# A retention layer with a gated feed-forward network on one core: fewer, wider column blocks in the middle of the feed-forward loop

## The chip, the core and the metric

The kernel runs on one core of a Trainium2 chip. The core has a matrix engine (TensorE, PE in the profile; its weight loads are PEld), three elementwise engines (VectorE is DVE, ScalarE is ACT, GpSimd is POOL), and a sync engine (SP) whose queue issues nearly all the DMAs. [...] The metric is the device time of one execution in microseconds.

## What is computed

Two layers, one fed into the other. First a retention layer: 8 batches, 8 heads, 576 positions, head size 64. Then a gated feed-forward network on its output, taken as 4608 rows (tokens) of 512 features, with 1536 hidden features.

```python
scores = scale * np.matmul(q, k.transpose(0, 1, 3, 2))
Dmat   = np.where(rel >= 0, gamma[:, None, None] ** rel[None, :, :], 0.0)
attn   = np.matmul(scores * Dmat[None, :, :, :], v)        # no softmax
x      = attn.transpose(0, 2, 1, 3).reshape(B * S, H * D)  # 4608 x 512
gate   = 1.0 / (1.0 + np.exp(-(x @ w_gate)))
out    = (gate * (x @ w_val)) @ w_out                      # 4608 x 512
```

Since there is no softmax, the retention layer is done chunk by chunk with a running state. The work within a chunk is a small masked product, and everything before the chunk enters through the state (the sum of k times v so far).

## The kernel before

**Columns.** The result of the retention layer is kept transposed in `xT`: 4 tiles of 128 features by 4608 columns, one column a token. Everything downstream counts in columns. Columns 0 to 768 are made by a special first part (three "pairs" of chunks). It also runs the feed-forward network on columns 0 to 512. The rest is done by the loop at the end of the kernel (lines 786 to 802), and that loop is what the change touches.

**The retention layer as steps.** The columns from 768 on are made by 34 steps, numbered from 0 (`STEPS`, line 68). A step is one chunk of one batch: 128 columns, or 64 for the last chunk of a batch ("short"; 576 is four chunks of 128 and one of 64). Steps 0 and 1 are full, 2 and 3 short, then each batch has four full ones and a short one. Step 4 begins at column 1152, step 7 at 1536, step 12 at 2112.

Each step has a supply side, which doesn't use TensorE:

- `load` (L105): v, k and q of the chunk come from memory, three DMAs on the SP queue.
- `cast_k` (L252), `cast_q` (L262), `cast_v` (L273), all on POOL: q and k are scaled by the decay tables and cast to bf16 into `qk_nat`, v into `vbd`. There are four of each buffer.
- `cross` (L289): a transposing DMA on the SP queue turns `qk_nat` into `T`, which holds q and k with the head dimension on partitions.

And it has a TensorE side of three or four **phases**: `st0` and `st1` add to the state (L432, not in a short step), `qk` makes the scores from `T` (L399), `pv` makes the output (L418 with the state, L420 within the chunk). DVE masks the scores (L401) and casts the state (L438). ACT casts the result into `xT` (L422) and prepares v (L283).

The order of the SP queue is written out by hand in `casts_to`: for each step x first the loads of step x + 1 (x + 2 from step 12 on), then, after the casts of k and q, the transpose of step x. The queue issues them in just this order.

**The feed-forward network as blocks.** `BLOCKS` (L786) cuts the columns from 512 on into blocks. For a block of n columns, `ffn_units` yields small units of TensorE work. In `h_units`, for each of 12 groups of hidden features there are four matmuls of n columns with the gate weights and four with the value weights (L495). ACT takes the sigmoid and DVE multiplies (L509 and L511 up to 256 columns, where gate and value share one PSUM buffer and are one unit; L519 and L523 above, with a buffer and a unit each). In `op_units`, for each 128 columns, 12 matmuls of 512 columns with the output weights (L561) follow in three units of four. ACT copies the result out (L538), and its store is issued once ten results are waiting. The PSUM ring for all of this has three buffers.

**How the two are interleaved.** While block w is computed, the loop puts in the phases that make the columns of block w + 1, since all of them must be in `xT` before block w + 1 can begin:

```python
end = upto(last_step(nxt[0] + nxt[1])) if nxt else len(order)
todo = end - at
total = 2 * NFC * 4 * n + 12 * 512 * (n // P)
...
    advance(begin + min(todo, -(-todo * gone // (total - 3 * 2048))))
```

`todo` is the number of phases due in this block. After each unit, `gone` of `total` matmul columns have been issued, and phases are let through in proportion, so that the last one comes shortly before the block ends. `order` is the fixed list of phases. It begins st0 0, qk 0, st1 0, pv 0, st0 1, qk 1, st1 1, qk 2, pv 1, qk 3, pv 2, pv 3, st0 4, qk 4 and so on. So the list of blocks sets two things: how many matmuls the hidden layer takes, and how early each phase stands in TensorE's stream. In the kernel before, the first block has the first 9 of these phases in it (up to pv 1), the second the next 11.

Of the kernel before, what the change touches and what calls it, by code (L numbers as in the profile page):

```python
# [16 lines left out]
def kernel(  # L17
# [22 lines left out]
    NT, DM = out.shape  # L40
# [489 lines left out]
    def leave():  # L530
        r, ob = stores.pop(0)
        for p0, r0, w in rows(r, P):
            nc.sync.dma_start(out[r0:r0 + w, :], ob[p0:p0 + w])
# [47 lines left out]
    def upto(s):  # L581

        return order.index(("pv", s)) + 1

    def last_step(t1):
        return max(s for s in range(NS) if at_col[s] < t1)
# [196 lines left out]
        nc.vector.memset(t, 0.0)  # L783
    casts_to(1)

    BLOCKS = [(512, 256), (768, 256)] + [(t, 384) for t in range(1024, 2560, 384)]  # L786
    BLOCKS += [(t, 512) for t in range(2560, NT, 512)]
    pieces = 0
    for w, (t0, n) in enumerate(BLOCKS):
        nxt = BLOCKS[w + 1] if w + 1 < len(BLOCKS) else None  # L790
        end = upto(last_step(nxt[0] + nxt[1])) if nxt else len(order)
# [4 lines left out]
        for cols in ffn_units(t0, n):  # L796
            gone += cols
            pieces += 1
            if stores and (nxt is None or w + 2 == len(BLOCKS) and pieces % 4 == 0):
                leave()  # L800
# [33 lines left out]
```

## Time and profile before

The median of three runs is 337.31 us (337.24 to 337.34). The profiled execution spans 335.4 us.

| engine | busy us | share | what most of it is |
|---|---|---|---|
| PE | 328.0 | 98% | L495 hidden layer, 960 matmuls; L561 output layer, 372 |
| POOL | 185.2 | 55% | L252 73.3 us, L273 47.4, L262 35.4: the casts of the steps |
| ACT | 167.8 | 50% | L519 52.2, L283 41.9 |
| DVE | 164.2 | 49% | L523 59.6, L438 43.7 |

The median of the transposing DMAs takes 4.3 us from issue to landing, that of the loads of k 4.6. Matmuls overlap in the pipeline: a matmul of 384 columns is listed with a mean near 330 ns, though the next one starts about 162 ns later. So the time that a matmul costs is read from the distance between starts, in the timeline, and not from its listed duration; and a PE that is busy 98% of the span isn't thereby known to be free of short waits.

The blocks can be found in the timeline of PE by the size of the L495 matmuls. The block at column 512 starts at 55.75 us, the one at 768 at 73.39, the ones of 384 columns at 91.44, 118.00, 144.5 and 169.7, and the first of 512 columns at 197.58.

### The profile page before, as it was taken

The numbers are of one execution on the slowest core, as the hardware profiler recorded it, in microseconds if no ns is written. First come the engines' busy times: TensorE is split into PE (matmuls) and PEld (weight loads), VectorE is DVE, ScalarE is ACT, GpSimd is POOL, SyncE is SP. The second block draws the span as 40 slices with busy tenths as digits, with TensorE's granted clock in tenths as the row PEclk, the third lists the DMA queues.
The fourth block names the chain that finished last, engine by engine and source line by source line (L and its number), as shares of the span: only waits on it lengthen the run. The fifth ranks groups of instructions, "written<-read, shape, count | busy, mean of one in ns | idle before, by whom it ended". The sixth has DMA issues, their size and how long they took to land.

```text
span 335.4 us, 7396 instructions
## 1 busy us (share of the span) xinstructions
PE 328.0 (98%) x2784; PEld 184.3 (55%) x2784; DVE 164.2 (49%) x328; ACT 167.8 (50%) x345; POOL 185.2 (55%) x327
## 2 busy tenths in 40 slices
PE   7999999999999999999999999999999999999996
PEld 3544445969666566556566555445555455444443
DVE  5744755726376356436346635542574156503320
ACT  6545635637565456355456655445646455233321
POOL 5655679779868798882448966582577500000000
PEclk9999999999999999999999999999999999999999
DMA  7999996799999999999976999499773850020002
GB/s 210 313 372 359 335 255 131 139 225 201 174 214 193 186 205 211 214 247 214 225 132 125 185 240 199 106 232 247 136 135 82 254 203 2 0 95 33 0 31 96
DMA packets 164100, 60.00 MB, mean 179 GB/s; under 512 B 144480, under 2 KB 156000, under 8 KB 164064
## 3 DMA queue, kind: packets, MB, share of 16 engines
q1 hardware_dynamic: 163920, 59.39, 83.2%
q8 instruction: 22, 0.36, 0.5%
q10 hardware_dynamic: 144, 0.13, 0.1%
q14 instruction: 14, 0.11, 0.1%
HBM read 37.75 MB, written 9.44 MB: 141 GB/s over the span
## 4 chain that ended last, share of the span: by engine, by line
PE 94%; DMA 2%; DVE 1%; SPq 1%; issue 1%; ACT 0%; POOL 0%
PE h L495 49%; PE op L561 24%; PE op L745 3%; PE hg L610 3%; PE hv L610 3%; PE pv L420 2%; PE qk L399 2%; PE pv L418 2%; DMA k32p<-in_k_dram 2%; PE st L432 2%; SPq L114 1%; PE op L551 1%; PE pvp L370 1%; PE idle L159 1%; PE st L345 0%
## 5 line engine op out<-in xcount | busy, mean ns | idle before, releaser
L495 PE MATMUL h<-xT,wg_sb 128*128 128x384 bf16 (+2 forms) x480 | 102.8, 337 | 0.2 <-DVE gv L523 0.2
L495 PE MATMUL h<-xT,wv_sb 128*128 128x384 bf16 (+2 forms) x480 | 102.8, 337 | 0.0
L252 POOL TENSOR_TENSOR qk_nat<-k,ktab 64x256 bf16<-64x256 f32 x120 | 73.3, 611 | 42.9 <-PE st L432 27.5
L523 DVE TENSOR_TENSOR gv<-g,h 128x384 bf16<-128x384 bf16 (+1 forms) x96 | 59.6, 621 | 71.8 <-PE h L495 56.4
L561 PE MATMUL op<-wo_sb,gv 128*128 128x512 bf16 x372 | 85.5, 379 | 0.0
L519 ACT ACTIVATE g<-h 128x384 bf16<-128x384 f32 (+1 forms) x96 | 52.2, 544 | 64.9 <-PE h L495 58.3
L438 DVE CAST sbd<-st 64x256 bf16<-64x256 f32 x104 | 43.7, 420 | 45.1 <-PE st L432 42.9
L495 PEld LDWEIGHTS <-wg_sb 128*128 128x128 bf16 x480 | 43.7, 98 | 31.4 <-issue 0.4
L495 PEld LDWEIGHTS <-wv_sb 128*128 128x128 bf16 x480 | 44.1, 98 | 29.0 <-issue 0.4
L273 POOL CAST vbd<-v 64x256 bf16<-64x256 f32 x120 | 47.4, 395 | 15.2 <-PE pv L420 10.6
L561 PEld LDWEIGHTS <-gv 128*128 128x128 bf16 x372 | 34.4, 98 | 36.3
L538 ACT COPY ob<-op 128x512 f32<-128x512 f32 x33 | 19.3, 585 | 47.5 <-PE op L561 42.8
L283 ACT CAST vs<-v 64x256 bf16<-64x256 f32 x104 | 41.9, 403 | 1.6
L262 POOL TENSOR_TENSOR qk_nat<-q,qtab 128x512 bf16<-128x512 f32 (+1 forms) x34 | 35.4, 1041 | 2.6
L422 ACT CAST xT<-pv 128x512 bf16<-128x512 f32 (+1 forms) x34 | 18.1, 534 | 18.1 <-PE pv L420 18.0
L401 DVE TENSOR_TENSOR pt<-qk,tri 128x512 bf16<-128x512 f32 (+1 forms) x34 | 21.2, 625 | 6.1 <-PE qk L399 5.8
L420 PE MATMUL pv<-pt,vbd 128*128 128x64 bf16 x240 | 18.0, 193 | 0.0
L432 PEld LDWEIGHTS <-qk_nat 128*128 128x128 bf16 x208 | 13.2, 98 | 8.8
L420 PEld LDWEIGHTS <-vbd 128*128 128x128 bf16 x240 | 15.2, 98 | 3.5
L418 PE MATMUL pv<-T,sbd 128*128 128x64 bf16 x216 | 17.2, 193 | 0.0
L511 DVE TENSOR_TENSOR gv<-g,h 128x256 bf16<-128x256 bf16 x24 | 10.0, 420 | 13.7 <-ACT g L509 13.3
L418 PEld LDWEIGHTS <-sbd 128*128 128x128 bf16 x216 | 15.1, 98 | 2.5
(76 smaller groups left out, 232.8 us busy)
## 6 DMA issues: line engine op xcount, KB each, us to landing
out_dram<-ob SPq DMA_DIRECT2D x34, 256.0 KB, 2.8
v<-in_v_dram SPq DMA_DIRECT2D x26, 256.0 KB, 4.1
k<-in_k_dram SPq DMA_DIRECT2D x26, 256.0 KB, 4.6
q<-in_q_dram SPq DMA_DIRECT2D x26, 256.0 KB, 5.1
wg<-in_moe_w_gate_dram SPq DMA_DIRECT2D x12, 256.0 KB, 6.0
wv<-in_moe_w_val_dram SPq DMA_DIRECT2D x12, 256.0 KB, 5.8
wo<-in_moe_w_out_dram SPq DMA_DIRECT2D x12, 256.0 KB, 5.4
k32p<-in_k_dram SPq DMA_DIRECT2D x6, 256.0 KB, 5.6
```

The source lines that it names most:

```text
L252: nc.gpsimd.tensor_tensor(out=kn[half(hh), j, :, half(hh)], in0=k32[half(j), hh::2, :], in1=ktab[half(j), c, hh::2].unsqueeze(2).to_broadc ...
L262: nc.gpsimd.tensor_tensor(out=qs[0:n], in0=q32[0:n], in1=qtab[0:n, c, :].unsqueeze(2).to_broadcast([n, H, D]), op=ALU.mult)
L273: nc.gpsimd.tensor_copy(out=vb[half(hh), j, :, half(hh)], in_=v32[half(j), hh::2, :])
L283: nc.scalar.copy(out=natural["vs", s][half(hh), j], in_=loaded[s][0][half(j), hh::2, :])
L401: nc.vector.tensor_tensor(out=pt[:, :, 0:n].rearrange("p m (j t) -> p m j t", t=64), in0=qkp[:, :, 0:n].rearrange("p m (j t) -> p m j t", ...
L418: nc.tensor.matmul(pvp[:, m, half(j)], lhsT=before[:, m, :], rhs=qT[:, m, half(j)], start=True, stop=False)
L420: nc.tensor.matmul(pvp[:, m, half(j)], lhsT=vb[:, j, m, :], rhs=pt[:, m, half(j)], start=before is None, stop=True)
L438: nc.vector.tensor_copy(out=sb[half(hh), :, half(hh)], in_=st_tiles[b][half(hh)])
L495: nc.tensor.matmul(out, lhsT=w_sb[:, kc, fc * P:(fc + 1) * P], rhs=xT[:, kc, t0 + a:t0 + e], start=(kc == 0), stop=(kc == NKC - 1))
L519: nc.scalar.activation(out=g[:, 0:n], in_=h1[:, 0:n], func=AF.Sigmoid)
L523: nc.vector.tensor_tensor(out=gvs[some[0]][:, a:e], in0=g[:, 0:n], in1=h2[:, 0:n], op=ALU.mult)
L561: nc.tensor.matmul(opp, lhsT=gvs[fc][:, nb * P:(nb + 1) * P], rhs=wo_sb[:, fc, :], start=(fc == 0), stop=(fc == NFC - 1))
```

## The change

The list of blocks is cut differently. Columns 768 to 2560 were one block of 256 and four of 384. Now they are two of 384 and two of 512. The block at 512 keeps its 256 columns, and from 2560 on both lists have the same four blocks of 512. The number of blocks falls from ten to nine. Wider blocks mean that each loaded weight tile is used for more columns, so the hidden layer takes fewer matmuls and weight loads, and ACT and DVE fewer instructions for the same columns. No other line is changed, and what is computed stays the same.

```diff
-    BLOCKS = [(512, 256), (768, 256)] + [(t, 384) for t in range(1024, 2560, 384)]
-    BLOCKS += [(t, 512) for t in range(2560, NT, 512)]
+    BLOCKS = [(512, 256), (768, 384), (1152, 384)] + [(t, 512) for t in range(1536, NT, 512)]
```

Since the loop takes the phases of block w + 1 into block w, the change also moves phases: the unchanged first block now has to let through all phases up to column 1152, where it was 1024.

## The prediction

> **What bounds the kernel now.** I read the page's busy times first. They put TensorE at 98% and every other engine near half:
>
> ```profile
> PE 328.0 (98%) x2784; PEld 184.3 (55%) x2784; DVE 164.2 (49%) x328; ACT 167.8 (50%) x345; POOL 185.2 (55%) x327
> ...
> PE   7999999999999999999999999999999999999996
> ```
>
> Next, the waits of PE alone, from 56 us (the first block of the loop) to 332. The answer has a single line:
>
> ```profile
> PE h L495 <- DVE gv L523: 0.2, 1, 0.2
> ```
>
> So in 276 us PE waits visibly once. Going by distances between starts in the PE timeline, small hesitations too short for this list add up to some 0.7 us. From 56 us on the kernel takes as long as PE needs to issue its matmuls; only fewer matmul cycles, or new waits, can move the end.
>
> Then I asked how close the other engines are to making PE wait. A `qk` phase needs its transpose `T`. PE's timeline around steps 1 and 2:
>
> ```profile
> 64.66 0.40 PE L399 MATMUL qk<-T 128*128 128x64 bf16 x8
> ...
> 66.64 0.28 PE L432 MATMUL st<-vs,qk_nat 128*128 128x64 bf16 x4
> ...
> 67.63 0.28 PE L399 MATMUL qk<-T 128*128 128x64 bf16 x4
> 67.75 1.89 PE L561 MATMUL op<-wo_sb,gv 128*128 128x512 bf16 x8
> ```
>
> The SP queue's timeline has the transposes of steps 2 and 3, with the loads between them:
>
> ```profile
> 61.98 1.69 SPq L105 DMA_DIRECT2D q<-in_q_dram  x1
> 63.78 1.28 SPq L289 DMA_TRANSPOSE T<-qk_nat  x1
> 65.11 0.59 SPq L105 DMA_DIRECT2D v<-in_v_dram  x1
> ...
> 67.87 1.73 SPq L289 DMA_TRANSPOSE T<-qk_nat  x1
> ```
>
> The DMA view of a window that holds one of these at a time gives 3.6 us to landing for step 2 and 4.1 for step 3. `T` of step 2 therefore lands at 63.78 + 3.6 = 67.4, and its `qk` starts at 67.63: **0.26 us to spare**, and nothing in the waits shows it. In the same way: steps 0 and 1 land at 57.1 and 62.65 (3.8 us each; used 57.61 and 64.66), step 3 at 71.95 (used 74.27), step 4 at 78.44 (79.38), step 5 at 83.6 (84.57), step 6 at 90.1 (93.50).
>
> Does PE hold this supply back? POOL's timeline says no:
>
> ```profile
> 62.93 0.83 POOL L273 CAST vbd<-v 64x256 bf16<-64x256 f32 x2
> 65.45 1.28 POOL L252 TENSOR_TENSOR qk_nat<-k,ktab 64x256 bf16<-64x256 f32 x2 [1.70 <-DMA k<-in_k_dram]
> ```
>
> From 49.5 to 63.8 us POOL casts without a gap; then it waits for the k of step 3, which was issued behind the transpose of step 1 at 61.34 and took 4.0 us. The next wait, 1.51 us before 70.12, is listed under PE pv L420, but the k load issued at 65.75 lands 4.2 us later, at 69.95, so I read it as the load again. The supply is a loop of SP issue, load, casts, issue, and up to step 12 it runs at its own pace.
>
> **What the Trainium skill says.** "TensorE: Matmul & The Clock Gate", section "Wait — 56ns, not 53.3ns?": a matmul of N columns takes N / 2.4 GHz plus about 2.5 ns, 215.7 ns at 512. The trace agrees: eight of 256 columns take 0.872 us (56.74 to 57.61), 109.0 ns each; four of 384 0.650, 162.5 each; four of 512 0.863, 215.8. Same page, "Step-by-step: what each phase is for": only weight loads are pulled ahead, matmuls "stay in program order". So a `qk` without its `T` stops the hidden-layer matmuls behind it; the trace before has no such stop to check it on. "DMA: Bandwidth & Descriptors", "Anatomy of one DMA — SWDGE (gpsimd) path": semaphore waits are served on the issuing sequencer, before dispatch. The trace agrees for SP: from 57.2 to 58.85 it issues nothing, waiting for POOL's q cast of step 1, though the loads of step 3 stand behind this transpose (issued from 60.35).
>
> **The change, part by part.**
>
> *Fewer matmuls.* Columns 768 to 2560 take 96 hidden-layer matmuls a block: five blocks before, four after. Before: 96 x (109.0 + 4 x 162.5) ns = 72.86 us. After: 96 x (2 x 162.5 + 2 x 215.8) = 72.63. **Gain 0.23 us.** The output layer (14 x 12 matmuls of 512) and the phases are the same ones. Weight loads (98 ns each, beside the matmuls), and the 12 sigmoids and 12 multiplies saved, lie beside PE at half load: nothing.
>
> *Phases earlier in the first block.* It has 18 units of 2048 columns, total 36864, so after unit u ceil(todo x u / 15) phases are through. todo goes from 9 to 12 (up to pv 3). Before, this puts qk 0, 1, 2 behind units 2, 9 and 12, as the timeline shows. After: qk 0, 1, 2, 3 behind units 2, 7, 9 and 12. From the start at 55.75, with 0.872 a unit (0.863 in the output layer), 0.117 for st, 0.235 for qk, 0.463 for pv (starts in the timeline; half for short steps):
> - qk 0 due at 57.61, as before; lands 57.1.
> - qk 1 due at 62.91 (was 64.66); lands 62.65. Just fits.
> - qk 2 due at 65.01 (was 67.63); lands 67.37. I add 0.2 for semaphore and weight load: POOL starts 0.13 to 0.16 after its loads land, a weight load takes 0.098. PE can go on at 67.57: **wait of 2.56 us**.
> - qk 3: 0.117 + two units + pv 1 + one unit = 3.20 later, due at 70.77; lands 71.95, go at 72.15: **wait of 1.38 us**.
>
> Sum 3.94. It is fixed by step 3 alone: unhindered, qk 3 would be due at 68.21. Behind the waiting qk stand all further hidden-layer matmuls, hence the whole rest of the kernel; nothing fills the hole. Up to here POOL and SP do what they did before, for PE gives them nothing they wait for.
>
> *After that.* The first block ends at 77.91 (73.39 before), and the same count gives: qk 4 due 79.98 (lands 78.44), qk 5 88.1 (83.6), qk 6 96.4 (90.1), qk 9 113.9 (105.5), qk 11 125.5 (118.0), qk 13 138.9 (133.5). The waits have bought the lead: at least 1.5 us to spare, later 5 to 8. The four step buffers come free in time too: POOL starts the k cast of step 8 at 92.54, st1 of step 4, which frees the buffer, is due near 82.
>
> *Heavy blocks.* Before, the block at 2176 holds 18 phases in 384 columns (0.37 us of hesitation near 179, behind ACT and DVE). Now 1152 does, with the same 18, so I let that recur; of the other 0.3 us, most of it in blocks of 384, I count 0.2 as gone. Both ends: 0 to 0.66 us gained.
>
> Sum: 337.31 + 3.94 - 0.23 - 0.2 = **340.8 us**, 1.0% slower.
>
> **Rivals.** (a) *The supply keeps up*, if the transposes are really in time by some reserve that I overlook, or land earlier since PE frees something sooner. For it: PE never waits for `T` in the trace. Against: 0.26 us of reserve where 2.6 are asked for, and POOL's gaps end with loads. Then only the gains stay: 337.31 - 0.23 - (0 to 0.66) = 336.4 to 337.1, likeliest 336.9. (b) *Only one wait*: step 3 lands earlier than before, its loads not sharing the DMA engines with as much; the wait at qk 2 stays. 337.31 + 2.56 - 0.43 = 339.4. Against: up to 66 us SP issues the same transfers at the same times. (c) *The waits cost more*: the skill's first page ("What's actually happening") has the clock halved after an idle window of about 3.4 us. One such window of 3.4 us at half rate would add 1.7 us: 342.5. Against: the waits are 2.6 and 1.4 us with 3.2 us of work between, and the clock row of the page reads 9 throughout. A stall in later steps, if the supply were also held back by PE's delay, would land here too.
>
> **How the numbers follow.** As forecast 0.75; (a) 0.08; (b) 0.07; (c) 0.10. The forecast case itself spans 340.2 to 341.4: 0.3 us on the landings (3.6 to 4.5 us for the first five), 0.3 on the small hesitations. The range takes most of (b) and the near half of (c): 339.3 to 342.2. Faster by over 0.2% means under 336.64, the better end of (a): 0.03. Same: the rest of (a), 0.05. Slower: 0.92.
>
> **What would show it.** PE's waits from 56 us on should list qk L399 waiting for the transposing DMA, twice, about 2.6 and 1.4 us, both before 73 us; the transposes of steps 2 and 3 should be issued within some tenths of 63.8 and 67.9; the 384-column matmuls should begin near 77.9 us, and L495 drop from 960 to 864 matmuls. From 80 us on PE should be without waits over half a microsecond. I am wrong if the transposes come much earlier, if the hole at qk 2 is missing, or if waits for `T` go on behind step 4.

## The result and the profile after

The changed kernel takes **339.47 us** in the median (four executions, 339.25 to 340.4), the kernel before 337.32. The ratio is 1.0068, with a 95% interval of 1.0049 to 1.0087; here and below it isn't just the quotient of the two medians. By the medians the kernel became slower by 2.15 us, where 3.5 were forecast. The profiled execution took 339.37 us and spans 337.7 us (335.4 before).

The first lines of the page, as shown of before:

```profile
PE 325.7 (96%) x2648; PEld 174.9 (52%) x2688; DVE 163.7 (48%) x316; ACT 166.1 (49%) x333; POOL 185.7 (55%) x327
...
PE   8899999789999999999999999999999999999996
```

The weight loads show the 96 matmuls that went (2784 - 96 = 2688). Of the matmuls themselves 40 records are missing, so the 325.7 us can't be set against the 328.0 of before: a second profile of the changed kernel (e12 below) has all 2688 and lists 328.4 us busy in a span of 338.0. In the row of 40 slices, the eighth place (59.1 to 67.5 us) falls to 7 and the ninth to 8.

The waits of PE alone, over the loop (56 to 332 us), have again a single line, but another one:

```profile
PE qk L399 <- DMA T<-qk_nat: 2.9, 2, 1.9
```

And these are the two waits, in PE's timeline (start, duration, and in brackets the idle time that went before):

```profile
64.32 0.60 PE L495 MATMUL h<-xT,wv_sb 128*128 128x256 bf16 x4
66.83 0.29 PE L399 MATMUL qk<-T 128*128 128x64 bf16 x4 [1.92 <-DMA T<-qk_nat]
...
69.61 0.60 PE L495 MATMUL h<-xT,wv_sb 128*128 128x256 bf16 x4
71.18 0.29 PE L399 MATMUL qk<-T 128*128 128x64 bf16 x4 [0.96 <-DMA T<-qk_nat]
```

Both rows have four matmuls, so they are the short steps 2 and 3. Since a matmul's listed end is modelled, I measure a hole between starts: the four matmuls from 64.32 on need 0.437 us of issue, so the next could start at 64.76, and it starts at 66.83. The hole is 2.08 us; the second, in the same way, 1.13. **Together 3.21 us.** All holes below are measured like this, on unrounded starts.

The supply runs nearly as it did before. The SP queue:

```profile
61.63 0.63 SPq L105 DMA_DIRECT2D q<-in_q_dram  x1
62.66 1.63 SPq L289 DMA_TRANSPOSE T<-qk_nat  x1
64.33 0.58 SPq L105 DMA_DIRECT2D v<-in_v_dram  x1
...
67.83 1.27 SPq L289 DMA_TRANSPOSE T<-qk_nat  x1
```

The transposes of steps 2 and 3 are issued at 62.66 and 67.83, where it was 63.78 and 67.87. That of step 2 is thus 1.1 us earlier: the q load in front of it held the queue for 0.63 us, where it was 1.69. The DMA view gives 4.1 and 3.3 us to landing (3.6 and 4.1 before), so they land at 66.8 and 71.1, and each `qk` starts 0.05 us after. Between 64.76 and 66.83 PE starts no matmul, although hidden-layer matmuls that need nothing from the transpose stand behind the `qk`. POOL has its gap as before, 2.01 us (1.70 before) ahead of the k cast of step 3, for the load of k.

**The account.** The span divides into three parts: up to the start of the loop, the holes at `qk`, and the rest. Before: 335.38 = 55.75 + 0 + 279.63. After: 337.66 = 55.49 + 3.21 + 278.96. So the waits cost 3.21 us, the rest became **0.67 us shorter**, and the loop began 0.26 us earlier. That last part isn't from the change: the program is the same up to there, in the profiles of this study the loop begins between 55.49 and 56.35, and in the second profile of the changed kernel at 55.91.

### The profile page after: what moved, and what is told of

Read it like the earlier page. It is cut to its first block, busy times and chain, and to the rows that moved or that the text cites. A ratio compares the mean times of both kernels' runs of the same rounds, so it can differ in the third digit from the quotient of the medians.

```text
span 337.7 us, 7133 instructions
## 1 busy us (share of the span) xinstructions
PE 325.7 (96%) x2648; PEld 174.9 (52%) x2688; DVE 163.7 (48%) x316; ACT 166.1 (49%) x333; POOL 185.7 (55%) x327
## 4 chain that ended last, share of the span: by engine, by line
PE 89%; DMA 3%; POOL 3%; issue 1%; DVE 1%; ACT 0%; SPq 0%; POOLq 0%; DVEq 0%
PE h L495 45%; PE op L561 23%; PE hg L610 3%; PE op L745 3%; PE hv L610 3%; PE qk L399 2%; PE pv L420 2%; PE pv L418 2%; PE st L432 2%; POOL qk_nat L252 1%; DMA k<-in_k_dram 1%; POOL vbd L273 1%; DMA q32p<-in_q_dram 1%; DMA T<-qk_nat 1%; PE idle L159 1%
## 5 line engine op out<-in xcount | busy, mean ns | idle before, releaser
L495 PE MATMUL h<-xT,wv_sb 128*128 128x512 bf16 (+2 forms) x422 | 99.8, 355 | 0.5
L495 PE MATMUL h<-xT,wg_sb 128*128 128x512 bf16 (+2 forms) x425 | 100.0, 355 | 0.4
L523 DVE TENSOR_TENSOR gv<-g,h 128x512 bf16<-128x512 bf16 (+1 forms) x96 | 62.8, 655 | 68.7 <-PE h L495 54.5
L519 ACT ACTIVATE g<-h 128x512 bf16<-128x512 f32 (+1 forms) x96 | 54.7, 570 | 70.5 <-PE h L495 68.2
L561 PE MATMUL op<-wo_sb,gv 128*128 128x512 bf16 x357 | 84.3, 379 | 0.7
L495 PEld LDWEIGHTS <-wg_sb 128*128 128x128 bf16 x432 | 39.4, 98 | 34.0
L495 PEld LDWEIGHTS <-wv_sb 128*128 128x128 bf16 x432 | 39.3, 98 | 31.6
L399 PEld LDWEIGHTS <-T 128*128 128x128 bf16 x240 | 11.4, 98 | 10.0 <-DMA T<-qk_nat 3.4
```

Source lines behind the costliest of these rows:

```text
L495: nc.tensor.matmul(out, lhsT=w_sb[:, kc, fc * P:(fc + 1) * P], rhs=xT[:, kc, t0 + a:t0 + e], start=(kc == 0), stop=(kc == NKC - 1))
L519: nc.scalar.activation(out=g[:, 0:n], in_=h1[:, 0:n], func=AF.Sigmoid)
L523: nc.vector.tensor_tensor(out=gvs[some[0]][:, a:e], in0=g[:, 0:n], in1=h2[:, 0:n], op=ALU.mult)
L561: nc.tensor.matmul(opp, lhsT=gvs[fc][:, nb * P:(nb + 1) * P], rhs=wo_sb[:, fc, :], start=(fc == 0), stop=(fc == NFC - 1))
```

## The experiments

Theory: the loss is the two waits, set by a supply that runs at its own pace; the wider blocks by themselves gain a little. Rivals: the wide blocks cost something themselves; POOL's casts alone hold the supply, or the k loads alone.

All ratios are taken beside the kernel before on the same chip. The columns from "profiled us" on belong to the one execution that was profiled, which can lie well off the median. "T3" is the landing of step 3's transpose in the trace, counted from the start of the loop; "rest" is the span less loop start and holes.

| run | median us | ratio (95%) | profiled us | loop start | T3 | holes at qk | rest |
|---|---|---|---|---|---|---|---|
| before | 337.3 | | 337.18 | 55.75 | 16.20 | 0 | 279.63 |
| changed | 339.47 | 1.0068 (1.0049 to 1.0087) | 339.37 | 55.49 | 15.64 | 3.21 | 278.96 |
| e1 | 341.5 | 1.011 (1.0091 to 1.0128) | 339.86 | 55.95 | 15.17 | 2.74 | 279.37 |
| e2 | 340.43 | 1.0088 (1.006 to 1.0116) | 339.03 | 55.88 | 16.01 | 2.17 | 279.27 |
| e3 | 342.17 | 1.0146 (1.0132 to 1.0161) | 341.82 | 56.05 | 17.51 | 5.07 | 278.96 |
| e4 | 341.31 | 1.0123 (1.0104 to 1.0142) | 341.31 | 55.60 | 17.45 | 5.01 | 278.96 |
| e5 | 339.26 | 1.006 (1.0042 to 1.0077) | 338.40 | 56.04 | 14.11 | 1.70 | 278.94 |
| e6 | 338.92 | 1.0052 (1.0038 to 1.0067) | 339.14 | 55.78 | 15.06 | 2.17 | 279.43 |
| e7 | 337.27 | 1.0001 (0.9993 to 1.0009) | 337.72 | 56.35 | 14.79 | 0 | 279.65 |
| e8 | 339.51 | 1.0066 (1.0052 to 1.008) | 339.45 | 56.03 | 15.64 | 2.73 | 278.98 |
| e9 | 337.42 | 1.0002 (0.9992 to 1.0012) | 337.41 | 55.69 | 15.60 | 0.95 | 279.03 |
| e10 | 338.19 | 1.0027 (1.0018 to 1.0035) | 338.23 | 55.95 | 15.20 | 1.48 | 279.07 |
| e11 | 340.06 | 1.0078 (1.0063 to 1.0093) | 341.03 | 55.91 | 16.46 | 4.01 | 279.40 |
| e12 | 339.65 | 1.0073 (1.0055 to 1.0091) | 339.75 | 55.91 | 15.55 | 3.12 | 278.97 |

**e1, the phases moved, the widths kept.**

```diff
+    BLOCKS = [(512, 256), (768, 384), (1152, 384), (1536, 384), (1920, 256), (2176, 384)]
+    BLOCKS += [(t, 512) for t in range(2560, NT, 512)]
```

> The list of blocks is 256, 384, 384, 384, 256, 384 and then four of 512: the same ten widths as in the kernel before, so just as many matmuls, but in an order that puts the phases up to column 1152 into the first block, as the change does. If the loss comes from the two waits for the transposes of steps 2 and 3, they show here with some 2.1 and 1.1 us, as in the changed kernel, and the time is 337.3 + 3.2, less up to 0.4 for small hesitations that may go: 340.1 to 340.5 us, that is slower than the changed kernel by the 0.2 us of 96 matmuls and a bit. If the loss comes from the wide blocks themselves (a ring of three PSUM buffers, later results), this kernel has no more of them than the kernel before and takes 337.3.

No block is wider than before and no matmul saved, yet the kernel is slower, with both waits in its profile (1.64 and 1.10 us):

```profile
66.85 0.29 PE L399 MATMUL qk<-T 128*128 128x64 bf16 x4 [1.47 <-DMA T<-qk_nat]
...
71.17 0.29 PE L399 MATMUL qk<-T 128*128 128x64 bf16 x4 [0.94 <-DMA T<-qk_nat]
```

So the loss goes with the phases in the first block and not with width. The rest is 279.37, above the changed kernel's 278.96. The times were not as expected: two of six executions took 339.9 to 340.0 us, four 341.5 to 341.7, and the profile is of one of the former. e11 comes back to this.

**e2, the widths alone.**

```diff
+    BLOCKS = [(512, 256), (768, 256)] + [(t, 512) for t in range(1024, NT, 512)]
```

> The list is 256, 256 and then seven blocks of 512: as many matmuls as in the changed kernel, one block of 512 more than it has, and the first block keeps its 9 phases. If supply is what counts, there is no wait at qk 2 and qk 3; but the second block now takes 15 phases, which brings qk 4, 5 and 6 forward to about 78.4, 82.9 and 87.3 us against landings of 78.3 to 78.4, 83.1 to 83.6 and 88.3 to 90.1 in the two traces: waits that add up to 1.4 to 3.0 us, all between 78 and 91 us, and a time of 338.2 to 339.9 us. If only the first block's phases mattered, 336.9. If width itself costs, at least the 339.5 of the changed kernel, with waits spread over the wide blocks behind 95 us.

No hole at qk 2 and qk 3; instead one at qk 5 (0.19 us) and one at qk 6:

```profile
90.00 0.41 PE L399 MATMUL qk<-T 128*128 128x64 bf16 x8 [1.81 <-DMA T<-qk_nat]
```

Profile as expected: the wait moves to where phases were moved. The median is 0.5 us above the expected range, but it lies between two groups. Three executions (338.73 to 339.53 us, the profiled one among them) had a granted TensorE clock of 1.000 and are inside the range; three took 341.33 to 341.70 us, and their clock was 0.995 in the mean. In e3 one execution of four (0.995) and in e4 two of five (0.994 and 0.990) had such a clock too, each time the slowest of their run; in all other runs no execution is below 0.998. The paragraph on the rivals comes back to this.

**e3, loads two steps ahead, in the changed kernel.**

```diff
-            loads_to(x + (1 if x < 12 else 2))
+            loads_to(x + 2)
```

> The changed kernel with the loads issued two steps ahead of the casts from step 0 on, where it is one step up to step 11. If the k load of step 3, issued behind the transpose of step 1, is what holds step 3, POOL's gap of 2.0 us before the k cast of step 3 goes, the transpose of step 3 is issued near 66 us and lands near 69.5, before its qk at about 70.0: the second wait (1.1 us) goes. Step 2 was held by POOL's own casts, so the first wait stays at about 2 us. Time 338.2 to 338.5. If POOL's pace alone holds both, or the loads only get slower for being more at a time, no change: 339.5.

Wrong: it became slower, with three holes in place of two. POOL did lose its gap. But the SP queue shows what it cost:

```profile
59.15 1.44 SPq L289 DMA_TRANSPOSE T<-qk_nat  x1
60.64 0.90 SPq L105 DMA_DIRECT2D v<-in_v_dram  x1
61.60 0.83 SPq L105 DMA_DIRECT2D k<-in_k_dram  x1
62.48 1.58 SPq L105 DMA_DIRECT2D q<-in_q_dram  x1
64.17 2.41 SPq L289 DMA_TRANSPOSE T<-qk_nat  x1
66.68 0.52 SPq L105 DMA_DIRECT2D v<-in_v_dram  x1
...
68.86 2.22 SPq L289 DMA_TRANSPOSE T<-qk_nat  x1
```

From 59 us on it issues without a pause, and one step's set takes 4.7 us (64.17 to 68.86). Counted from the start of the loop, step 3's transpose is issued 0.47 us later than in the changed kernel, and it flies 1.4 us longer (4.7 us in place of 3.3), which makes up the 1.87 us in T3. The transpose of step 1 takes 5.6 us to landing (3.8 before); why isn't shown, for in e12 it takes as long with the loads in their old places. PE then waits for steps 1, 2 and 3:

```profile
64.75 0.41 PE L399 MATMUL qk<-T 128*128 128x64 bf16 x8 [1.38 <-DMA T<-qk_nat]
68.82 0.29 PE L399 MATMUL qk<-T 128*128 128x64 bf16 x4 [1.79 <-DMA T<-qk_nat]
73.60 0.29 PE L399 MATMUL qk<-T 128*128 128x64 bf16 x4 [1.41 <-DMA T<-qk_nat]
```

**e4, the same, and the casts of v of steps 0 and 1 off POOL.**

```diff
-            cast_v(x)
+            if x > 0: cast_v(x, on_dve if x == 1 else on_pool)
...
-    cast_dense(0, 1)
+    cast_dense(0, 1); cast_v(0, on_act)
```

> The changed kernel with loads two steps ahead and with the casts of v of steps 0 and 1 taken off POOL (step 0 to ACT, where it is idle near 53 us, step 1 to DVE near 55 us). POOL then reaches the casts of steps 2 and 3 some 3.4 us sooner. If the two waits are all that the change costs, both go, and its gains are left: 0.23 us for 96 matmuls and 0 to 0.66 us of hesitations, 336.5 to 337.1 us. If the wider blocks cost something by themselves, the time stays above 337.5 with no wait for a transpose in it.

Wrong in the same way, with holes of 0.46, 2.90 and 1.65 us at qk 0, 2 and 3, and it says more. POOL has finished the q cast of step 2 at 60.6 us, but its transpose is issued at 63.60, behind the loads of step 4. From POOL's timeline and SP's:

```profile
59.59 1.04 POOL L262 TENSOR_TENSOR qk_nat<-q,qtab 64x512 bf16<-64x512 f32 x1
...
61.57 1.92 SPq L105 DMA_DIRECT2D q<-in_q_dram  x1
63.60 2.40 SPq L289 DMA_TRANSPOSE T<-qk_nat  x1
```

POOL 2 us faster gained nothing here, with the loads in the queue in front of the transpose. So the k loads alone don't hold the supply (e3), nor did POOL's relief show with the loads ahead: the supply is a loop of queue, DMA and POOL, and in these two runs relief at one member was lost at the next.

**e5, only the casts of v moved. e6, also the loads in the order k, q, v.**

```diff
-        for nm, src in (("v", v), ("k", k), ("q", q)):
+        for nm, src in (("k", k), ("q", q), ("v", v)):
```

> The changed kernel with the casts of v of steps 0 and 1 off POOL (to ACT and DVE), the loads in their old places: the runs with earlier loads showed the SP queue issuing without a pause and the transposes stuck behind the loads, so supply is to be sped up without putting more in front of a transpose. POOL's k cast of step 2 then waits for its load (59.1 us) and not for POOL; transposes of steps 2 and 3 are issued near 61.5 and 65.8 and land near 65.5 and 69.5, against qk due at 64.8 and 68.0 (start of the loop at 55.5). Waits of about 0.8 and 0.7 us in place of 2.1 and 1.1; time 1.7 us under the changed kernel: 337.6 to 338.2. If POOL's casts have no part in it, 339.5 as before; if the other engines' queues suffer, PE waits for ACT or DVE in the first block.

> As the run before, and each step's loads issued in the order k, q, v, so that the k cast, which POOL does first, gets its data some 0.9 us sooner. The transposes of steps 2 and 3 should land near 64.6 and 68.6: at most 0.6 us of waits in all are left. Then the gains of the change show: 0.23 us of matmuls and some of the hesitations of blocks of 384: 336.6 to 337.4 us, not slower than the kernel before. If wider blocks cost something themselves, above 338 without waits for transposes.

Half right. In e5 the hole at qk 2 is gone, as expected, but qk 3 still waits: its transpose is issued at 65.70 as forecast and takes 4.5 us, not 3.7, so 1.70 us are left of 3.21. POOL's casts do have a part in the supply, then, but not the only one. In e6 the transpose of step 3 is issued only at 66.46, though POOL is done at 65.6: the loads stand in front. Waits for transposes 2.17 us; another 0.46 for DVE, which has a cast of v more, sits in the rest (279.43 - 0.46 = 278.97). The profile of e5 is of its fastest execution (338.40 us), so 1.70 is a good draw. The medians, 339.26 and 338.92, gained little over the changed kernel's 339.47.

**e7, these two edits in the kernel before.**

> The kernel before with the same two edits of the supply (casts of v of steps 0 and 1 moved, loads in the order k, q, v). It had no waits for transposes to lose: 337.0 to 337.5 us, no change but a narrower scatter. The distance to the same supply with the changed blocks is then the change without its waits: forecast -0.2 to -0.6 us. If the supply edits gain by something else than these waits, this one gains as much as the changed kernel does.

No change, as expected: 1.0001. It had no wait to lose. Its rest of 279.65, against e6's 278.97 without the wait for DVE, puts the change without its waits at -0.68 us, a little beyond the -0.2 to -0.6 expected.

**e8, the demand moved instead of the supply.**

```diff
-            advance(begin + min(todo, -(-todo * gone // (total - 3 * 2048))))
+            advance(begin + min(todo, -(-todo * gone // (total - (3 if w else 1) * 2048))))
```

> The changed kernel with its supply as it is, but the 12 phases of the first block spread over 17 of its 18 units and not over 15: qk 2 stands behind unit 10 and not 9, qk 3 behind 13 and not 12, each asked for 0.87 us later. The transposes are issued and land as before. If the waits are demand against a supply that PE does not move, their sum falls by just this, from 3.2 to 2.3 us, and the time by 0.9: 338.4 to 338.8. If PE's later demand also lets the supply come later, or the loss is elsewhere, 339.5.

T3 is 15.64, to the hundredth as in the changed kernel. That is partly chance: the transpose is issued 0.59 us earlier against the loop's start and flies 0.59 us longer (3.9 us). The holes at qk 2 and qk 3 are 0.83 + 1.52 = 2.35 us where 2.3 were forecast, so asking later didn't make the supply later. But a third hole opens, at qk 4 (0.38 us), which was not forecast, and this loop began 0.54 us later. In time nothing was won: 339.51 us. The 0.5 us less of holes in all is inside the scatter of the ratio (1.0052 to 1.008).

**e9 and e10, attempts at a version that beats both.** e9 has the blocks of e2, the supply of e6, and the second block's phases spread over 17 of its 18 units. e10 has the changed blocks, the casts of e5, and in the first two blocks nothing kept free at the end (`total - (3 if w > 1 else 0) * 2048`).

> An attempt at a version that beats both: nine blocks (256, 256, seven of 512), so the first block keeps its 9 phases; the casts of v of steps 0 and 1 off POOL and the loads in the order k, q, v; and the 15 phases of the second block spread over 17 of its 18 units. Counted from the start of the loop, qk 4, 5 and 6 are due at 22.7, 28.0 and 32.4 us; with these supply edits the transposes landed at 21.2 to 21.5, 25.6 to 26.0 and 31.5 to 33.1. Waits of 0 to 0.7 us in all. If the waits are all that stands against fewer matmuls: 0.23 us less for the matmuls, up to 0.5 less for hesitations of the 384 blocks, 336.6 to 337.5 us, level with the kernel before or a shade under. If width itself costs, above 338.

> The changed blocks (256, 384, 384, then 512) with the casts of v of steps 0 and 1 off POOL, and with the phases of the first two blocks spread over the whole block, with no units kept free at the end. From the start of the loop qk 2, 3 and 4 are due at about 11.0, 14.5 and 20.9 us; with the casts moved the transposes landed at 9.2, 14.1 and 21.2. So about 0.3 us of waits, where the changed kernel has 3.2, and 336.7 to 337.6 us. If a wait grows elsewhere (the last phase of the first block is now followed by one unit only, before the next block needs its columns), PE shows it at the start of the second block, waiting for ACT's xT.

In e9 one hole is left, 0.95 us at qk 6 (0 to 0.7 expected), against 2.17 us in e2:

```profile
89.21 0.41 PE L399 MATMUL qk<-T 128*128 128x64 bf16 x8 [0.78 <-DMA T<-qk_nat]
```

It is level with the kernel before (1.0002). e10 has 1.48 us of holes (1.06 at qk 3, the rest at qk 4) where 0.3 were expected, and stays 0.3% slower, outside the expected range: T3 was 15.20, where I had put 14.1. Neither beats the kernel before.

**e11 and e12, e1 and the changed kernel again.**

> The list 256, 384, 384, 384, 256, 384, then 512, once more. Its executions fell into two groups, two near 339.9 us and four near 341.6, and the profile was of the lower one. If the upper group comes from the same place, its profile shows larger waits of PE for the transposes of the first steps, by about 1.6 us in sum (a supply that starts or runs later against the loop), and nothing new behind 95 us. If it is something else, the waits are 2.7 us as in the first profile and the 1.6 us lie in a later loop start or in later blocks.

> The changed kernel itself, beside the kernel before on this chip. Four executions gave 339.25 to 340.4. With the waits of the first profile 339.3 to 339.6 again; if the transposes land as they did in the profile of the kernel before (3.6 and 4.1 us after an issue at the same distance from the loop's start), the waits are 3.7 to 3.9 us and the time 340 to 340.4. PE's waits must again be two, at the qk of steps 2 and 3.

The profile of e11 is of its slowest execution (341.03 us; the other three 339.95 to 340.16), and has four holes, one more at each earlier step:

```profile
64.78 0.41 PE L399 MATMUL qk<-T 128*128 128x64 bf16 x8 [1.28 <-DMA T<-qk_nat]
68.11 0.29 PE L399 MATMUL qk<-T 128*128 128x64 bf16 x4 [1.06 <-DMA T<-qk_nat]
72.42 0.29 PE L399 MATMUL qk<-T 128*128 128x64 bf16 x4 [0.93 <-DMA T<-qk_nat]
```

With 0.25 us at qk 0 that is 4.01, 1.27 more than in e1, and the executions are 1.17 us apart. POOL began step 0 at 50.40 us with the loop at 55.91, so 5.51 us ahead of it, where it was 6.61 us ahead in e1: the supply started 1.1 us late against the loop, which is most of the 1.27. The four slower executions of e1 itself have no profile. e12 has 3.12 us of holes, at qk 1, 2 and 3: three, not two. There POOL began at 49.56, 6.35 us ahead of the loop and much as in the first profile (6.31), but the transpose of step 1 took 5.6 us to land. That moved a part of the wait forward to qk 1 and left the sum as it was. What sets the start of the supply and the flight times from one execution to the next stays open.

**One formula.** By the units and phases of the changed first block, qk 3 is due 12.46 us after the loop's start if nothing waits (68.21 - 55.75 in the prediction). The waits up to there should add up to T3 + 0.05 - 12.46. For changed, e1, e3, e4, e5, e11, e12 this gives 3.23, 2.76, 5.10, 5.04, 1.70, 4.05, 3.14; measured were 3.21, 2.74, 5.07, 5.01, 1.70, 4.01, 3.12. For e8, with 0.87 more, 2.36 against 2.35. Once qk 3 starts right behind the landing, this is bookkeeping. What it shows is that in every one of these runs the landing of step 3 released qk 3, and that PE lost next to nothing up to there but at a `qk`. In e6 the formula gives 2.65, and the holes are 2.17 and the 0.46 for DVE.

## Why the prediction was right, and where it was off

*What bounds the kernel, and what was a hair from bounding it.* Right. The step that decided was to compare each transpose's landing with its use: 0.26 us to spare at step 2, while no list of waits showed it. The experiments bear it out: e1 has the waits without the wide blocks, e2 has them where its phases were moved, and e8 shortens the first two by what was forecast.

*Phases earlier.* Right in place and kind: qk 2 and qk 3, for the transposing DMA, and no hole at a `qk` after 80 us. That there were just two was luck: at qk 1 the transpose landed 0.08 us before its use, where 0.26 was forecast, and in e12 PE waits there too. The reserve at qk 4 was 0.72 us and not 1.5, mostly because the shorter waits brought qk 4 forward by 0.7 us while its transpose landed no earlier against the loop; e8 used it up. **The term that was mis-sized is the sum of the waits, 3.94 us, measured 3.21.** I carried T3's landing over from the trace before, 16.20 us after the loop's start; it was 15.64 (3.3 us of flight in place of 4.1, after an issue 0.22 us later). That is 0.56. The short flight isn't from the change, for e2, which keeps the first block's 9 phases, has 3.3 us too. The allowance of 0.2 us from landing to start was 0.05: another 0.15. e11, with a landing at 16.46 and 4.01 us, and e12, with 15.55 and 3.12, show that one trace gives one draw of it. The range had 0.3 us for the landings, and the forecast case alone was to span 340.2 to 341.4. The measured 339.47 lies below that, 0.17 us inside the whole range, which reached so low only because it took in most of (b).

One of the signs named beforehand failed: the transpose of step 2 was issued at 62.66 and not within some tenths of 63.8. In the trace before, a slow q load had held it back by 0.8 us (POOL's q cast was done at 62.97). A longer flight (4.1 us for 3.6) took back more than half of the gain, and the sum of the waits is set by step 3 alone.

*The start of the loop*, 0.26 us earlier in the profiled execution, was in no step, since nothing in the program moves it.

*Fewer matmuls and hesitations.* Forecast 0.23 + 0.2 = 0.43 us, measured together 0.67. The hesitations outside the `qk` holes were 0.66 us before, 0.37 of that at one place:

```profile
178.26 0.81 PE L495 MATMUL h<-xT,wv_sb 128*128 128x384 bf16 x4
179.28 0.65 PE L495 MATMUL h<-xT,wg_sb 128*128 128x384 bf16 x3 [0.21 <-DVE gv L523]
```

I let this one recur in the new heavy block of 384 columns at 1152. It did not; that block has one of 0.19 us near 110. In e12, where no matmul record is missing, this is the only one left, and its rest is 278.97. So 0.47 us of hesitations went, and 0.2 remain for the matmuls, for which 0.23 was forecast. The matmuls were sized right, the hesitations at less than half of what they were.

*The sum*: 3.21 - 0.67 - 0.26 = 2.28 us of span, in place of 3.94 - 0.43 = 3.51.

*The rivals.* (a) fell: the reserve was as small as it looked. (b), one wait only, didn't come, though its 339.4 us is the time measured; both waits are there, only shorter. A part of what (b) named did happen: step 3 landed earlier, by 0.56 us against the loop's start. (c): no clock penalty in the changed kernel, after holes of 2.08 and 1.13 us; its ten executions have a granted clock of 0.999 to 1.000. The section "What's actually happening" of the Trainium skill's page "TensorE: Matmul & The Clock Gate" puts the idle window at about 3.4 us, and the holes of all the profiles stay below it; the longest, 2.90 us in e4, doesn't slow the clock either. But (c) isn't out for e2, e3 and e4, whose six executions with a clock of 0.990 to 0.995 have no profile. By an estimate from these figures, 0.5% of 340 us is 1.7 us, as much as (c) reckoned for one such window at half rate. Whether longer holes slowed those executions isn't shown.

## What to carry to other kernels

Before moving work earlier on the bounding engine, list for each item when its input lands and when it is used: a kernel without waits can be 0.26 us from its first one. Where the supply is a loop through a DMA queue, an engine and back, relieving one member can make it worse (e3). Moving the demand changed the first waits by just the amount forecast (e8), but then the next item waited (qk 4). And a landing time from one trace is one draw: here the same landing, counted from the loop's start, moved by up to 1.3 us between two profiles of one kernel.

## What the runs showed of the hardware

The transposing DMA of step 1 took 3.7 to 5.6 us from issue to landing, that of step 3 3.3 to 4.9, and each held the issuing queue for 1.3 to 2.6 us. In e3 and e4 those of steps 2 and 3 (4.6 to 4.8 us) stood close behind loads; the two of 5.6 us, at step 1 in e3 and e12, did not, so the cause isn't settled. PE resumed 0.05 us after a landing, where I had allowed 0.2. Six executions of e2, e3 and e4 had a mean granted clock of 0.990 to 0.995 and were the slowest of their runs.
